# Last keys of a head pair in four 64x64 tiles with half of the queries each, sums side by side, three raw weights in the gates' buffers

## The chip, the cores and the metric

The kernel runs on one core of one Trainium2 chip. A core has TensorE (PE, matrix products; its weight loads are listed as PEld), VectorE (DVE), ScalarE (ACT), GpSimd (POOL) and SyncE (SP, which issues DMAs), all with their own instruction streams. The metric is the device time of one execution in microseconds (us); lower is better.

## The reference

All inputs and the output are float32 or float64 as given: B = 4 batches, H = 12 heads, S = 448 tokens, D = 64 per head; the three FFN weights arrive as 64-bit floats and the kernel converts them itself.

```python
scores = (1 / sqrt(D)) * q @ k.T                   # per batch and head
scores = cap * tanh(scores / cap)
attn = exp(scores - max); attn = attn / (sum(attn) + 1e-9)
x = (attn @ v) as [B * S, H * D]                   # 1792 x 768
out = ((x @ w_a) * (x @ w_b)) @ w_out              # 768 -> 1536 -> 768
```

## The kernel before

**Pairs.** Heads are done two at a time: a pair is head `hp` and head `hp + 6` of one batch, 24 pairs in all. The transposed keys and queries of one head of the pair lie on rows 0 to 63 (the 64 numbers of a head), those of the other on rows 64 to 127; `own` names these two row halves. The 448 keys of a head make three tiles of 128 (c = 0 to 2) and a rest of `R` = 64, the last keys (c = 3).

**A pair's steps.** `scores` (L258) puts keys against queries, so a score tile has keys on its rows and 448 queries along it: per full tile one 128-column matmul for each head (L266), for the last keys one 64x64 tile for each head, where the two heads share one 128-row result. `tanh` (L277) and `exp` (L285) run on ScalarE, one exp for tiles 0 and 1 (half 0) and one for tiles 2 and 3 (half 1). `attend` (L301) multiplies values by the exponentials: 64 columns of values for each head, over 128 keys; the last keys of both heads lie in one 128-row tile, and `vb` holds zeros where the other head's rows are. The softmax sums need a sum over keys: VectorE adds the tiles (`add_full`, L289), and `sums` (L320) lets TensorE add up the 128 rows with a matrix of ones, 64 queries at a time (`SC`), 14 small matmuls in four column groups of 32. For pairs 3 to 11 (`ON_PE`) the last keys' part of that is done by seven more such matmuls, `sums_last` (L310), right behind attend; for the other pairs VectorE does it (`add_last`, L296). `recip`, a round through DRAM (`store_rec`, `load_den`) and `scale` divide; `split_x` writes x as a high and a low part.

**Two phases.** Pairs 0 to 11 (phase one) are attention alone, in fp32. Pairs 12 to 23 (phase two) run between pieces of the FFN's first half (the tokens of batches 0 and 1); there keys and queries are split in a high and a low part (`turn_hi`, `turn_lo`), and each score tile is three products of the faster fp32r type (L271); the last keys are copied into two zero-padded 128x128 tiles `kz` by ScalarE (`last_keys`, L251) and take three products of 128x128 (L274). After pair 23 the second half of the FFN runs alone. A piece of FFN is `hidden` (L455, 18 matmuls: 6 row blocks by three products) or `project` (L486, 9 matmuls over three blocks of `w_out`); `gate` (L469) multiplies the two hidden results and splits the product into high and low, in buffers with the tags `gh` and `gl`, three of each. Two of those six are lent out until then as `den` buffers of pairs 10 and 11 (`LENT`).

**Weights.** Each block of 128 x 768 is loaded as 64-bit floats (`load64`, L385, two buffers tagged `w64`), converted in six steps (`conv`, L402: two on ScalarE L406 and L409, three on VectorE L411, L414, L417, one on GpSimd L420), then split into a high part (`split_hi`, L433, on ScalarE in the first half) and a low part (`split_lo`, L448, VectorE). The blocks go in the order a0, b0, a1, b1, a2, b2, o0, o1, o2, and so on; `t` counts them. The program's names are `wta` and `wtb` for the converted block, `wha`, `wla` for its parts.

**What sets the order.** TensorE's order is written out in `chain` (L637 to 703): per pair of phase one the scores of tiles 0 and 1, attend of the pair before, the scores of tiles 3 and 2, sums of the pair before that; in phase two attend, scores 0 and 1, sums, FFN work of half a `GAP` (20.4 us), scores 3 and 2, FFN work again. For the other engines a planner at the end places each step by a due time that it counts back from the chain (`due`), with planned costs in us that stand in each `job`. The lines touched by the change are in `load_v`, `last_keys`, `scores`, `tanh`, `add_last`, `attend`, `sums_last`, `sums`, `load_den`, `load64`, `split_hi`, `gate`, and in the code that makes the jobs.

Of the kernel before, what the change touches and what calls it, by code (L numbers as in the profile page):

```python
# [119 lines left out]
def kernel(  # L120
# [29 lines left out]
    SC = 64  # L150
# [5 lines left out]
    AHEAD = 4  # L156
    BLK = 32
# [12 lines left out]
    even.tile([P, 688], F32, tag="even", name="even")  # L170
# [22 lines left out]
    kz = [const.tile([P, P], F32R, tag=f"kz{x}", name=f"kz{x}") for x in "hl"]  # L193
    vb = [const.tile([P, 2 * NC3 + 2, D], F32, tag=f"vb{i}", name=f"vb{i}") for i in range(3)]

    own, krem = (slice(0, D), slice(D, P)), (S - R, 0)
# [25 lines left out]
    def load_v(pi, n):  # L222
        b, hp = divmod(pi, NP)
        t = vb[pi % 3]
        j = n % 2
        src = v[b, hp + j * NP]
        eng = nc.gpsimd if 3 <= pi < NPG else nc.sync
        if n < 2:
            rows = src[j * R : j * R + NC3 * P].rearrange("(c p) d -> p c d", p=P)
            eng.dma_start(t[:, j * (NC3 + 2) : j * (NC3 + 2) + NC3], rows)  # L230
        else:
            eng.dma_start(t[own[j], NC3 + j], src[krem[j] : krem[j] + R])
# [12 lines left out]
    def turn_lo(pi, nm):  # L245
# [3 lines left out]
        stk[nm, pi] = (hi, lo)  # L249

    def last_keys(pi):  # L251
        for z, x in zip(kz, stk["k", pi]):
            for j, o in enumerate(own):
                nc.scalar.copy(z[o, j * R : (j + 1) * R], x[o, krem[j] : krem[j] + R])
# [3 lines left out]
    def scores(pi, c):  # L258
        tk, tq = stk["k", pi], stk["q", pi]
        psc = ps_sc.tile([P, 2, 512], F32, tag="pssc", name=f"psc_{pi}_{c}")  # L260
        full = c < NC3
        if pi < NPG:
            for j, o in enumerate(own):
                at = j * R + c * P if full else krem[j]
                to = psc[:, j, :S] if full else psc[o, 0, :S]
                nc.tensor.matmul(to, tk[o, at : at + (P if full else R)], tq[o], start=True, stop=True)  # L266
        elif full:
            for x, y in products:
                for j, o in enumerate(own):
                    kk = tk[x][o, j * R + c * P : j * R + (c + 1) * P]  # L270
                    nc.tensor.matmul(psc[:, j, :S], kk, tq[y][o], start=(x + y == 0), stop=(x == 1))  # L271
        else:
            for x, y in products:
                nc.tensor.matmul(psc[:, 0, :S], kz[x], tq[y], start=(x + y == 0), stop=(x == 1))  # L274
        prob[pi, "s", c] = psc

    def tanh(pi, c):  # L277
# [18 lines left out]
    def add_last(pi):  # L296
        t, pf = psum[pi % 2], prob[pi, 1]
        for j, o in enumerate(own):
            nc.vector.scalar_tensor_tensor(t[o, j], pf[o, 2], capt[o, 2:3], t[o, j], op0=ALU.add, op1=ALU.add)

    def attend(pi, hf):  # L301
# [3 lines left out]
        for c in range(2 * hf, 2 * hf + 2):  # L305
            for j, o in enumerate(own):
                p = prob[pi, hf][:, 2 * (c % 2) + (j if c < NC3 else 0)]
                nc.tensor.matmul(t[o, :S], tv[:, j * (NC3 + 1) + (c if j == 0 else (c + 1) % (NC3 + 1))], p, start=(c == 0), stop=(c == NC3))  # L308

    def sums_last(pi):  # L310
        t, pf = pvs[pi], prob[pi, 1]
        for m in range(0, SUB, 2):
            for i in range(P // Q):
                c = 2 * i + m // 2
                if c < NSC:
                    to = t[i * Q : (i + 1) * Q, S : S + SC]
# [592 lines left out]
```

## Time and profile before

| | |
|---|---|
| three runs, us | median 720.1, from 717.47 to 720.37 |
| the profiled execution, us | 719.65 |
| its span in the trace, us | 717.5 |
| busy TensorE, us | 705.0 (98%) |
| busy VectorE / ScalarE / GpSimd, us | 427.7 / 347.3 / 112.4 |

Matmuls are pipelined and their ends are modelled, so TensorE's busy share overstates; the starts of instructions are to be used instead. An fp32 matmul has two records of TensorE in the trace for each matmul in the code (counts such as x8 for four). Names are those of the program with buffer numbers left out: `psc` is a score result, `pf` the exponentials, `pv` the result of attend (sums go into its last columns), `pha` and `phb` the two hidden results, `po` the projection's.

### The profile page before, as it was taken

What the parts mean: (1) busy time and instruction counts of PE and PEld (TensorE: products, weight loads), DVE (VectorE), ACT (ScalarE), POOL (GpSimd) and SP (SyncE); (2) the same over time, 40 slices, a digit from 0 to 9 for tenths busy, and PEclk for the clock granted to TensorE, in tenths of its full rate; (3) what the DMA queues carried; (4) which work ended last, traced back from release to release, by engine and by line L of the source; (5) the groups of instructions that cost most, each with busy time, mean ns of one, the idle gap of its engine ahead of it and who ended that gap; (6) DMA issues with size and microseconds to landing.
All of it is one profiled execution on the core that took longest, in us unless ns stands there. A gap on an engine that the chain in (4) does not pass through costs nothing.

```text
span 717.5 us, 11286 instructions
## 1 busy us (share of the span) xinstructions
PE 705.0 (98%) x4388; PEld 581.1 (81%) x4388; DVE 427.7 (60%) x651; ACT 347.3 (48%) x475; POOL 112.4 (16%) x104
## 2 busy tenths in 40 slices
PE   8999999999999999999999999999999999999996
PEld 4333367877877878878889779999999999999996
DVE  5777898867568689596795749342033434434232
ACT  6988987656866764686556530222321112202100
POOL 0445532222222222221231100000000000000000
PEclk9999999999999999999999999999999999999999
DMA  9997686775795678767654438331032003101012
GB/s 128 164 169 157 146 216 133 189 187 140 187 212 144 182 168 210 192 160 195 146 138 125 145 93 266 100 107 46 5 86 81 27 29 104 50 18 44 1 45 113
DMA packets 142597, 90.55 MB, mean 126 GB/s; under 512 B 107882, under 2 KB 128394, under 8 KB 142538
## 3 DMA queue, kind: packets, MB, share of 16 engines
q1 hardware_dynamic: 135786, 82.53, 46.3%
q0 software_dynamic: 3040, 6.79, 4.2%
q10 hardware_dynamic: 3712, 0.46, 0.5%
q8 instruction: 36, 0.59, 0.4%
q14 instruction: 23, 0.19, 0.1%
HBM read 67.24 MB, written 22.50 MB: 125 GB/s over the span
## 4 chain that ended last, share of the span: by engine, by line
PE 66%; DMA 13%; DVE 7%; ACT 7%; SPq 4%; issue 3%; POOL 1%; DVEq 0%; ACTq 0%; POOLq 0%
PE po L493 7%; PE po L495 7%; PE po L494 7%; PE pv L308 6%; PE pha L462 5%; PE pha L460 5%; PE pha L461 5%; PE phb L462 5%; PE phb L460 5%; PE phb L461 5%; PE psc L266 4%; DMA w64b<-in_moe_w_b_dram 3%; DMA w64o<-in_moe_w_out_dram 3%; DMA den<-rd 2%; ACT pf L283 2%
## 5 line engine op out<-in xcount | busy, mean ns | idle before, releaser
L493 PE MATMUL po<-who,gh 128*128 128x384 f32 x336 | 114.6, 341 | 2.6 <-ACT who L440 1.2
L494 PE MATMUL po<-wlo,gh 128*128 128x384 f32 x336 | 113.0, 336 | 0.6 <-DVE wlo L448 0.6
L495 PE MATMUL po<-who,gl 128*128 128x384 f32 x336 | 113.2, 337 | 0.1
L460 PE MATMUL pha<-xhi,wha 128*128 128x448 f32 x288 | 105.0, 365 | 0.0
L460 PE MATMUL phb<-xhi,whb 128*128 128x448 f32 x288 | 104.8, 364 | 0.0
L462 PE MATMUL pha<-xhi,wla 128*128 128x448 f32 x288 | 104.5, 363 | 0.0
L462 PE MATMUL phb<-xhi,wlb 128*128 128x448 f32 x288 | 104.5, 363 | 0.0
L461 PE MATMUL pha<-xlo,wha 128*128 128x448 f32 x288 | 104.3, 362 | 0.0
L461 PE MATMUL phb<-xlo,whb 128*128 128x448 f32 x288 | 104.2, 362 | 0.0
L283 ACT ACTIVATE pf<-psc,capt 128x896 f32<-128x896 f32 (+1 forms) x96 | 84.0, 909 | 17.4 <-PE psc L271 10.5
L308 PE MATMUL pv<-pf,vb 128*64 128x448 f32 x384 | 77.7, 546 | 0.8 <-ACT pf L287 0.8
L287 ACT ACTIVATE pf<-pf,capt 128x1792 f32<-128x1792 f32 (+1 forms) x48 | 77.2, 1608 | 0.8
L504 DVE TENSOR_TENSOR acc<-po,acc 128x384 f32<-128x384 f32 x84 | 46.2, 553 | 44.3 <-PE po L495 44.2
L493 PEld LDWEIGHTS po<-who,gh 128*128 128x128 f32 x336 | 63.6, 189 | 6.3 <-ACT who L440 1.5
L467 ACT COPY asb<-pha 128x448 f32<-128x448 f32 x48 | 25.5, 532 | 80.9 <-PE pha L462 80.9
L477 DVE TENSOR_TENSOR asb<-phb,asb 128x448 f32<-128x448 f32 x48 | 29.8, 621 | 58.5 <-PE phb L462 58.4
L494 PEld LDWEIGHTS po<-wlo,gh 128*128 128x128 f32 x336 | 63.7, 189 | 0.9 <-DVE wlo L448 0.8
L495 PEld LDWEIGHTS po<-who,gl 128*128 128x128 f32 x336 | 63.5, 189 | 0.4 <-DVE gl L482 0.4
L308 PEld LDWEIGHTS pv<-pf,vb 128*64 128x64 f32 x384 | 25.3, 136 | 45.3 <-issue 35.4
L479 ACT CAST gh<-asb 128x448 fp32r<-128x448 f32 x48 | 27.1, 564 | 69.1 <-DVE asb L477 68.7
L460 PEld LDWEIGHTS pha<-xhi,wha 128*128 128x128 f32 x288 | 53.9, 187 | 5.1 <-issue 0.6
L460 PEld LDWEIGHTS phb<-xhi,whb 128*128 128x128 f32 x288 | 53.9, 187 | 5.0 <-issue 1.2
(108 smaller groups left out, 1045.1 us busy)
## 6 DMA issues: line engine op xcount, KB each, us to landing
w64o<-in_moe_w_out_dram SPq DMA_DIRECT2D x24, 384.0 KB, 4.9
w64a<-in_moe_w_a_dram SPq DMA_DIRECT2D x18, 384.0 KB, 4.4
w64b<-in_moe_w_b_dram SPq DMA_DIRECT2D x18, 384.0 KB, 4.2
den<-rd SPq DMA_DIRECT2D x48, 112.0 KB, 3.9
out_dram<-acc SPq DMA_DIRECT2D x13, 384.0 KB, 3.8
wda<-wta SPq DMA_DIRECT2D x12, 384.0 KB, 6.3
wdb<-wtb SPq DMA_DIRECT2D x12, 384.0 KB, 5.5
wdo<-wto SPq DMA_DIRECT2D x12, 384.0 KB
```

The lines of the kernel that those rows point to most:

```text
L266: nc.tensor.matmul(to, tk[o, at : at + (P if full else R)], tq[o], start=True, stop=True)
L283: nc.scalar.activation(to, prob.pop((pi, "s", c))[:, :n, :S], AF.Tanh, scale=capt[:, 1:2])
L287: nc.scalar.activation(pf, pf, AF.Exp, scale=capt[:, 0:1])
L308: nc.tensor.matmul(t[o, :S], tv[:, j * (NC3 + 1) + (c if j == 0 else (c + 1) % (NC3 + 1))], p, start=(c == 0), stop=(c == NC3))
L460: nc.tensor.matmul(t[:, :S], wh[:, kk], xhi[:, kk, cs], start=(kk == 0), stop=False)
L461: nc.tensor.matmul(t[:, :S], wh[:, kk], xlo[:, kk, cs], start=False, stop=False)
L462: nc.tensor.matmul(t[:, :S], wl[:, kk], xhi[:, kk, cs], start=False, stop=(kk == NK - 1))
L477: nc.vector.tensor_mul(t, phs.pop(("b", h))[:, :S], t)
L493: nc.tensor.matmul(t[:, :HALF], gh[:, cs], wh, start=(f == fs[0]), stop=False)
L494: nc.tensor.matmul(t[:, :HALF], gh[:, cs], wl, start=False, stop=False)
L495: nc.tensor.matmul(t[:, :HALF], gl[:, cs], wh, start=False, stop=(f == fs[-1]))
L504: nc.vector.tensor_add(acc[:, ti, hs], t, acc[:, ti, hs])
```

## The change

- **Scores.** In phase one each full tile is now four 64x64 matmuls instead of two of 64x128 (row half by column half). The last keys are four 64x64 tiles too, in both phases: head j's 64 keys against the first 224 queries (`SH`) give rows 0 to 63 of the result's part j, and against the other 224 rows 64 to 127. In phase two these four are fp32 products from the unsplit keys and queries, which `stk` now keeps; `kz`, `last_keys` and its jobs are gone.
- **Attend, adds, tanh of the last keys** follow that layout: `vb` has two slots for each half of the queries, attend's last step is four matmuls of 224 columns instead of two of 448.
- **Sums.** `SC` is 56 instead of 64: `sums` has 16 matmuls, `sums_last` 8, and `sums_last` stands behind the scores of tile 2, next to `sums` of the pair before.
- **Weights.** `gh` and `gl` become one buffer of twice the length, tag `g`, three of them. Raw weights a0, b0 and a2 (t = 0, 1 and 4) are loaded into these before the gates need them, so the `w64` buffers have less to hold. The high parts of a0 and b0 are made on VectorE (`EARLY`). `LENT` is gone, so the `den` of pairs 10 and 11 wait for the two ordinary buffers.
- **Planner.** Planned costs and kinds follow (`sums_last` counts as `sums`). The turn of a phase-two pair waits for the scores of tile 3 of the pair before.

```diff
@@ constants @@
-    SC = 64
+    SH = S // 2
+    SC = 56
+    EARLY = 2
+    GRAW = (0, 1, 4)
...
@@ turn_lo, scores @@
-        stk[nm, pi] = (hi, lo)
+        stk[nm, pi] = (hi, lo, tt)
...
+        if c == NC3:
+            kk, qq = (t[-1] for t in (tk, tq)) if pi >= NPG else (tk, tq)
+            for i in range(2):
+                for j, o in enumerate(own):
+                    nc.tensor.matmul(psc[own[i], j, :SH], kk[o, S - R :], qq[o, i * SH : (i + 1) * SH], start=True, stop=True)
+        elif pi < NPG:
+            for i in range(2):
+                at = c * P + i * D
+                for j, o in enumerate(own):
+                    nc.tensor.matmul(psc[own[i], j, :S], tk[o, at : at + D], tq[o], start=True, stop=True)
...
@@ attend @@
+            for i in range(1 if c < NC3 else 2):
+                for j, o in enumerate(own):
+                    if c < NC3:
+                        nc.tensor.matmul(t[o, :S], tv[:, j * NC3 + c], prob[pi, hf][:, 2 * (c % 2) + j], start=(c == 0), stop=False)
+                    else:
+                        to = t[o, i * SH : (i + 1) * SH]
+                        nc.tensor.matmul(to, tv[:, 2 * (NC3 + i) + j], halves(prob[pi, 1][:, 2])[:, j], start=False, stop=(i == 1))
...
@@ load64, split_hi @@
+            if t in GRAW:
+                own_g = gp.tile([P, 2 * GT], F32R, tag="g", name=f"w64{nm}_{f}", bufs=GF)
+                wraw[t] = own_g[:, : 2 * DM].bitcast(I32).rearrange("p (n t) -> p n t", t=2)
...
-        if g and nm == "b":
+        if t < EARLY or g and nm == "b":
             nc.vector.tensor_copy(hi, wfull[t])
...
@@ turns, attend_of, the chain @@
+            free = [("scores", pi - 2, c) for c in range(SUB)] + [("lo", nm, pi - 1)] + [("scores", pi - 1, NC3)] * (pi > NPG)
...
-        if pi in ON_PE and 1 in halves:
-            on_pe(("sums_last", pi), 0.35, sums_last, (pi,))
...
+        if pi - 1 in ON_PE:
+            on_pe(("sums_last", pi - 1), 0.3, sums_last, (pi - 1,), [("exp", pi - 1, 1)])
         if pi > 1:
             sums_of(pi - 2)
```

The first place is TensorE in one pair of phase one (pair 5's scores). Before:

```order
L266 MATMUL psc_0_457<-tq_421,tk_413 128x448 x2
L266 MATMUL psc_1_467<-tq_421,tk_413 128x448 x2
L308 MATMUL pv_472<-pf_0_406,vb_175 64x448 x4
L308 MATMUL pv_472<-pf_1_436,vb_175 64x448 x4
L318 MATMUL pv_472<-pf_1_436,both 32x64 x7
L266 MATMUL psc_3_502<-tq_421,tk_413 64x448 x2
L266 MATMUL psc_2_509<-tq_421,tk_413 128x448 x2
L329 MATMUL pv_401<-psum_165,sel 32x64 x14
```

After:

```order
L267 MATMUL psc_0_578<-tq_499,tk_491 64x448 x4
L267 MATMUL psc_1_589<-tq_499,tk_491 64x448 x4
L309 MATMUL pv_596<-pf_0_518,vb_174 64x448 x4
L309 MATMUL pv_596<-pf_1_548,vb_174 64x448 x2
L312 MATMUL pv_596<-pf_1_548,vb_174 64x224 x4
L262 MATMUL psc_3_621<-tq_499,tk_491 64x224 x4
L267 MATMUL psc_2_630<-tq_499,tk_491 64x448 x4
L320 MATMUL pv_596<-pf_1_548,both 32x56 x8
L329 MATMUL pv_512<-psum_166,sel 32x56 x16
```

The small matmuls of `sums_last` moved from behind attend to directly ahead of `sums`, and all score tiles have 64 rows of result.

The second place is ScalarE, where the first steps of weight a0 (`w64a_0`, `wta_0`) stand between the tanh and exp steps. Before, in pair 7:

```order
L283 ACTIVATE pf_7_0_708<-psc_7_1_697,capt_132 128x896
L406 ACTIVATE w64a_0_419<-w64a_0_419 128x768
L287 ACTIVATE pf_7_0_708<-pf_7_0_708,capt_132 128x1792
L409 ACTIVATE wta_0_740<-w64a_0_419 128x768
L283 ACTIVATE pf_7_1_746<-psc_7_3_736,capt_132 128x448
```

After, in pair 9:

```order
L282 ACTIVATE pf_9_0_961<-psc_9_1_948,capt_132 128x896
L406 ACTIVATE w64a_0_450<-w64a_0_450 128x768
L286 ACTIVATE pf_9_0_961<-pf_9_0_961,capt_132 128x1792
L282 ACTIVATE pf_9_1_995<-psc_9_3_979,capt_132 128x448
L282 ACTIVATE pf_9_1_995<-psc_9_2_986,capt_132 128x896
L409 ACTIVATE wta_0_1035<-w64a_0_450 128x768
L286 ACTIVATE pf_9_1_995<-pf_9_1_995,capt_132 128x1344
```

The steps stand two pairs later. In the same way b0 moved from pair 8 to pair 10, a1 from pair 10 to pair 11.

The third place is VectorE at the end of phase one, up to the low part of b0 (`wlb_0_0`). Before, behind the second add of pair 10:

```order
L294 TENSOR_TENSOR psum0_165<-psum0_165,pf_10_1_991 128x896
L358 TENSOR_TENSOR den_7_984<-pv_7_783,den_7_984 128x448
L414 TENSOR_SCALAR wta_1_1021<-wta_1_1021 128x768
L374 CAST xhi_170<-den_7_984 128x448
L375 TENSOR_TENSOR xlo_171<-den_7_984,xhi_170 128x448
L448 TENSOR_TENSOR wlb_0_0_1080<-wtb_0_933,whb_0_0_1059 128x768
```

After, behind the first steps of pair 12 and the second add of pair 11:

```order
L250 TENSOR_TENSOR lq_12_1318<-tq_12_1226,hq_12_1289 128x448
L414 TENSOR_SCALAR wta_1_1277<-wta_1_1277 128x768
L293 TENSOR_TENSOR psum1_166<-psum1_166,pf_11_1_1244 128x896
L438 CAST whb_0_0_1342<-wtb_0_1142 128x768
L417 SCALAR_TENSOR_TENSOR wta_1_1277<-w64a_1_976,wta_1_1277 128x768
L448 TENSOR_TENSOR wlb_0_0_1373<-wtb_0_1142,whb_0_0_1342 128x768
```

The low part of b0 moved from pair 10's add to behind pair 11's, and its high part (`whb`) is now a step of VectorE.

## Rows read from the trace of the kernel before

**Rows 1.** The page: chain of work that ended last, share of the span by engine.

```profile
PE 66%; DMA 13%; DVE 7%; ACT 7%; SPq 4%; issue 3%; POOL 1%; DVEq 0%; ACTq 0%; POOLq 0%
```

**Rows 2.** Timeline, TensorE, one pair (start, duration, engine, line, operation, out<-in, shapes, count).

```profile
49.04 1.77 PE L266 MATMUL psc<-tq,tk 64*128 64x448 f32 x8
50.74 3.23 PE L308 MATMUL pv<-pf,vb 128*64 128x448 f32 x16
53.90 0.42 PE L318 MATMUL pv<-pf,both 128*32 128x64 f32 x14
54.26 1.92 PE L266 MATMUL psc<-tq,tk 64*64 64x448 f32 x8
56.11 0.65 PE L329 MATMUL pv<-psum,sel 128*32 128x64 f32 x28
56.68 0.65 PE L266 MATMUL psc<-tq,tk 64*128 64x448 f32 x2
```

**Rows 3.** Timeline, weight loads of that pair; brackets hold idle time and releaser.

```profile
51.17 0.14 PEld L308 LDWEIGHTS pv<-pf,vb 128*64 128x64 f32 x2 [0.23 <-issue]
51.55 0.14 PEld L308 LDWEIGHTS pv<-pf,vb 128*64 128x64 f32 x2 [0.23 <-issue]
...
55.15 0.30 PEld L266 LDWEIGHTS psc<-tq,tk 64*128 64x128 f32 x4 [0.70 <-ACT pf L287]
```

**Rows 4.** Timeline, ScalarE, at the start and in that pair.

```profile
8.10 1.91 ACT L283 ACTIVATE pf<-psc,capt 128x896 f32<-128x896 f32 x2 [1.75 <-PE psc L266]
...
21.22 1.89 ACT L283 ACTIVATE pf<-psc,capt 128x896 f32<-128x896 f32 x2
...
55.27 0.64 ACT L283 ACTIVATE pf<-psc,capt 128x448 f32<-128x448 f32 x1 [0.62 <-PE psc L266]
56.22 1.01 ACT L283 ACTIVATE pf<-psc,capt 128x896 f32<-128x896 f32 x1 [0.32 <-PE psc L266]
```

**Rows 5.** Timeline, ScalarE, first conversion step of weights a0 and b0.

```profile
60.37 0.92 ACT L406 ACTIVATE w64a<-w64a 128x768 int32<-128x768 uint32 x1
...
72.56 0.93 ACT L406 ACTIVATE w64b<-w64b 128x768 int32<-128x768 uint32 x1
```

**Rows 6.** Timeline, TensorE, two and one sums ahead of the first two FFN pieces.

```profile
94.72 1.09 PE L329 MATMUL pv<-psum,sel 128*32 128x64 f32 x56
95.74 0.48 PE L460 MATMUL pha<-xhi,wha 128*128 128x448 f32 x1
...
104.48 0.65 PE L329 MATMUL pv<-psum,sel 128*32 128x64 f32 x28
105.06 0.47 PE L460 MATMUL phb<-xhi,whb 128*128 128x448 f32 x1
```

**Rows 7.** Timeline, VectorE and ScalarE, steps at the end of phase one.

```profile
92.41 0.54 DVE L414 TENSOR_SCALAR wta<-wta 128x768 int32<-128x768 int32 x1
...
93.84 0.95 DVE L448 TENSOR_TENSOR wlb<-wtb,whb 128x768 fp32r<-128x768 f32 x1
...
97.73 0.59 ACT L242 CAST hq<-tq 128x448 fp32r<-128x448 f32 x1
...
99.61 0.61 DVE L248 TENSOR_TENSOR lq<-tq,hq 128x448 fp32r<-128x448 f32 x1
100.15 1.08 DVE L294 TENSOR_TENSOR psum<-psum,pf 128x896 f32<-128x896 f32 x1
```

**Rows 8.** Timeline, TensorE, last keys of a phase-two pair and what follows.

```profile
217.57 0.37 PE L274 MATMUL psc<-hq,kzh 128*128 128x448 f32 x1
...
218.27 0.47 PE L271 MATMUL psc<-hq,hk 64*128 64x448 f32 x2
```

**Rows 9.** TensorE in the first projection: timeline, then windows (busy, clock, DMA, GB/s).

```profile
162.75 0.44 PE L493 MATMUL po<-who,gh 128*128 128x384 f32 x1 [1.19 <-ACT who L440]
163.75 0.44 PE L494 MATMUL po<-wlo,gh 128*128 128x384 f32 x1 [0.55 <-DVE wlo L448]
...
160.00:168.00 8.00, 6.26 (x26) 5.44 (x23) 5.46 (x9) 6.62 (x10) 0.00 (x0) 0.79 0.65 182
```

More of the change, by code (lines that the diff above doesn't have):

```diff
@@ L192 @@
     acc = const.tile([P, NTI, DM], F32, tag="acc", name="acc")
-    kz = [const.tile([P, P], F32R, tag=f"kz{x}", name=f"kz{x}") for x in "hl"]
-    vb = [const.tile([P, 2 * NC3 + 2, D], F32, tag=f"vb{i}", name=f"vb{i}") for i in range(3)]
-    own, krem = (slice(0, D), slice(D, P)), (S - R, 0)
+    vb = [const.tile([P, 2 * NC3 + 4, D], F32, tag=f"vb{i}", name=f"vb{i}") for i in range(3)]
+    own = slice(0, D), slice(D, P)
     raw, stk, prob, pvs = {}, {}, {}, {}
@@ L260, in scores, with halves @@
         psc = ps_sc.tile([P, 2, 512], F32, tag="pssc", name=f"psc_{pi}_{c}")
[L261 to L267, printed above, removed]
+        if c == NC3:
[9 more added lines that the diff above has]
+        else:
             for x, y in products:
                 for j, o in enumerate(own):
[L270 to L274, printed above, removed]
+                    nc.tensor.matmul(psc[:, j, :S], tk[x][o, c * P : (c + 1) * P], tq[y][o], start=(x + y == 0), stop=(x == 1))
         prob[pi, "s", c] = psc
+    def halves(t):
+        return t.rearrange("p (j s) -> p j s", j=2)
     def tanh(pi, c):
@@ L297, in add_last @@
         t, pf = psum[pi % 2], prob[pi, 1]
-        for j, o in enumerate(own):
-            nc.vector.scalar_tensor_tensor(t[o, j], pf[o, 2], capt[o, 2:3], t[o, j], op0=ALU.add, op1=ALU.add)
+        for i, o in enumerate(own):
+            to = t[o, :, i * SH : (i + 1) * SH]
+            nc.vector.scalar_tensor_tensor(to, halves(pf[o, 2]), capt[o, 2:3], to, op0=ALU.add, op1=ALU.add)
     def attend(pi, hf):
@@ L353 @@
     xs, hold = {}, {}
-    LENT = {NPG - 2: "gh", NPG - 1: "gl"}
     def scale(pi):
@@ L558, in softmax @@
         job(("rd", pi), "SP", 0.7, store_rec, (pi,), [("recip", pi)], 3.0)
-        own_den = [p for p in range(pi) if p not in LENT]
-        free = [("x", own_den[-2])] if pi not in LENT and len(own_den) > 1 else []
+        free = [("x", pi - 2)] if pi > 1 else []
         for j in range(2):
@@ L692 @@
         attend_of(pi - 1)
+        if pi == NPG:
+            on_pe(("sums_last", pi - 1), 0.3, sums_last, (pi - 1,), [("exp", pi - 1, 1)])
         if pi < NPAIR:
@@ L794 @@
     for key in chain:
-        now = "ffn" if key[0] in ("hidden", "project") or (key[0] == "scores" and key[1:] >= (NPG, 3) and key[2] == 3) else key[0]
+        now = "ffn" if key[0] in ("hidden", "project") else "sums" if key[0] == "sums_last" else key[0]
         if now != kind:
```

86 lines of the change are left out of this document (34 added, 52 removed).

## The prediction

> **What bounds the kernel now.** I read the chain that ended last first: TensorE has 66% of it, the rest lies in pieces under 15% [rows 1]. So a gain has to come out of TensorE's own row, and I read that row by start times, since the ends of matmuls are modelled. The reader should take one pair of phase one from [rows 2]. From the start of its scores at 49.04 to that of the next pair at 56.68 it takes 7.64 us, in five groups without a wait: scores of tiles 0 and 1, 1.70; eight attend steps, 3.16; `sums_last`, 0.36; scores of tiles 3 and 2, 1.85; `sums`, 0.57. In that same pair ScalarE waits for scores twice, 0.62 and 0.32 us [rows 4]: TensorE is ahead of nothing there, it is the limit, and ScalarE has 0.94 us to spare. At the start it is the other way: ScalarE runs from 8.10 to 21.22 without a pause, two pairs in 13.12, so 6.56 a pair [rows 4]. That is the floor under any faster TensorE. In phase two TensorE waits for weights in a few places only; the worst is the first projection [rows 9].
>
> **What one group costs.** An fp32 matmul has two passes. In attend a pass starts every 0.38 us (51.17 to 51.55 [rows 3]); eight make 3.01 of the 3.16, so 0.15 us is lost where the tile shape changes. Scores with 128 columns on each 64-row half have four passes, 1.50, and take 1.70. The 64x64 scores of tile 3 take 0.89 for two passes, 0.14 over 0.75 (54.26 [rows 2] to 55.15 [rows 3]), like attend and not like the wide tiles. For sums, one alone takes 0.58 and two in a row take 1.02 (94.72 to 95.74, and 104.48 to 105.06 [rows 6]); so the second costs 0.44 for its eight steps of four tiles, 0.055 a step, and the change of shape 0.14.
>
> **The change, phase one.** Four tiles of 64x64 are not in the trace as a group. If all four run beside each other, as the two diagonal ones do, a pass of 448 columns stays at 0.38 and one of 224 costs 0.19 (on the line between 64 columns, 0.055, and 448, 0.376). If the two column halves of a row half take turns, each pass costs twice that. I take the first: two row halves beside each other (L266) and two column halves (L308) both show it, and nothing shows a limit on both at once.
> - Scores 0 and 1: four passes plus 0.16 for the change of shape and two more issues, 1.66 for 1.70: 0.04 less.
> - Scores 3 and 2: 2 x 0.19 + 2 x 0.376 + 0.16 = 1.29 for 1.85: 0.56 less; one change of shape falls away too, as tiles 3 and 2 now have the same.
> - `sums_last` beside `sums`: 24 matmuls for 21, but of 56 columns, in 12 steps at 0.049, plus 0.14: 0.73 for 0.93, so 0.20 less.
> - Attend: the last two passes become four of 0.19: nothing, at most 0.01 more.
> Together 0.80, so 6.84 us a pair, still over ScalarE's 6.56. In the slot of pair 3, where `sums_last` is not yet there, 7.29 (7.64 less 0.35) becomes 6.63.
>
> The start gains nothing, as ScalarE is the limit; it loses an estimated 0.3, half of a tanh of tile 3, since that of pair 0 now stands ahead of the exp that attend waits for. Tanh of pair 3 so starts at 21.22 + 6.56 + 0.3 = 28.1, that of pair 9 at 28.1 + 6.63 + 5 x 6.84 = 68.9. From there the conversions of weights stand in ScalarE's order, two instructions each (0.92 by the row, 0.8 each to the next start, so 1.6 [rows 5]): a0 in pair 9, b0 in pair 10, a1 in pair 11; before they stood two pairs earlier and used the 0.94 of spare time. Now ScalarE is the limit: exp of pair 10 ends at 68.9 + 2 x 6.56 + 2 x 1.6 = 85.2. Behind it TensorE has half an attend (1.58), scores 3 and 2 (1.29), and 20 steps of sums with a change of shape (1.12): the first FFN piece starts at 89.2. I take 89.5 for joints, against 95.74 [rows 6]: **6.2 us earlier**.
>
> **What is late next.** The second piece, phb, comes 9.3 us after the first [rows 6], at 98.8. Its weights must pass VectorE, whose order there has add and split steps of pairs 7 to 11 and now also the hi split of a0 and b0. Exp of pair 11 ends at 85.2 + 6.56 + 1.6 = 93.4; behind it ScalarE makes two hi parts of pair 12 (0.59 each by its row), so lq of pair 12 starts on VectorE at 94.6, and then come six steps up to wlb: lq 0.54 and add 1.00 (to the next start), a step of the shift's kind 0.54 and the hi split like it, L417 and L448 0.95 each [rows 7]. That is 4.52, so wlb is done at 99.1 with nothing lost at a handover. So phb waits 0.3 by the count; I take 0.9, since the pieces behind it have no slack either, and 5.3 us is left.
>
> **Phase two.** Tile 3 of scores was three 128x128 products, 0.70 us to the next group with its change of shape (217.57 to 218.27 [rows 8]), and had no change of shape ahead of it. Now there is one ahead (0.09) and four fp32 tiles of 224 columns: 0.09 + 2 x 0.19 + 0.14 = 0.61, 0.09 less. Sums of 8 steps at 0.049 instead of 0.055: 0.05 less. Twelve pairs: 1.6 us. The four copies of last keys a pair leave ScalarE; I count no gain for it, since TensorE's waits in the trace are for weights. The turn of the next pair now waits for the scores of tile 3 of the last one; half a `GAP` of FFN work (10.2 us as planned) and an attend lie between, and its chain is three steps of about 0.6 each.
>
> The first projection now stands idle 1.19 us for who and 0.55 for wlo, and the eight us around that have a granted clock of 0.79 of full speed on average, so the lower of its two levels (1.2 instead of 2.4 GHz) for part of them [rows 9]: 1.74 idle and 0.21 x 8 = 1.7 of clock, 3.4 us in all. Raw weights come earlier after the change (three more buffers), but demand comes 5 us earlier too, and the conversion of the second output weight stands later in ScalarE's order, behind exp of pair 14. Bounds: all 3.4 us gained, or as much lost again. I take 0.7 gained.
>
> **Sum.** The profiled execution took 719.65 with a span of 717.5, and the runs had a median of 720.1. 719.65 - 5.3 - 1.6 - 0.7 = **712.0 us**. The second half of the FFN is as it was.
>
> **A rule to weigh.** In attend the weight load of the next pass runs (0.14 us) while the current pass streams in the same 128 rows, and passes keep 0.38 apart [rows 3].
> The Trainium skill, TensorE: Matmul & The Clock Gate, Part 3 (The mechanism), says that a weight load overlaps running matmuls only when its row group differs. By that rule the column halves of one row half would each show their load. The trace disagrees for tiles of 128 rows; for four of 64x64 no run here shows it.
> If loads did show, eight passes a pair would each be 0.13 longer (a load of 64 columns on 64 rows lies near attend's 0.14), 12.8 us in twelve pairs: 724.8.
>
> **Rivals.**
> 1. *Conversions keep their length.* For: VectorE and ScalarE are full at the seam, and from its first ScalarE step [rows 5] to the end of its low part [rows 7] weight b0 took 22.2 us (72.56 to 94.79). With its start after the change at 79.0 (68.9 + 6.56 + 1.6 and two tanh, 1.9), b0 is done at 101.2, and phb waits 2.4 to 2.8, not 0.9; the backlog goes on to the first projection, which loses 3 more than now. That is 1.9 + 3.7 more than in the forecast: 717.6, within 0.5%. Against: much of those 22 us was lying idle for a due time.
> 2. *Column halves take turns* (ends slower). Place: the scores of phase one. Price: 0.75 for each of three tiles and 0.38 for the fourth, per pair 2.63, 31.6 in phase one and 4.5 in phase two, 748. It cancels the gain once a fifth of the passes are doubled. For: two streams of queries read the same 64 rows. Against: attend's two streams do so on 128 rows and hold 0.38.
> 3. *Loads show*, as above: 724.8.
> 4. *The change does not do what it says*, if four tiles or 56-column steps cost what the old ones did and only shape changes fall away (0.15 a pair in nine pairs, and nothing else): 718.
>
> **How the numbers follow.** Forecast 71%, rival 1 16%, rival 2 5%, rival 3 4%, rival 4 4%. About 0.5% (3.6 us) is what a measurement of this kernel can tell from no change, so faster means under 716.5. All but a little of the forecast is there: 0.70 faster; rivals 1 and 4 and that little make 0.20 within it; rivals 2 and 3, with some of a worse projection, 0.10 slower. The range reaches down to the forecast with the whole projection stall gone and the phb wait gone too, with joints 1 us better (712.0 - 2.7 - 0.9 - 1.0, about 707), and up past rivals 1 and 4 to 718.5.
>
> **What would show it.** Right: a pair of phase one in 6.8 to 6.9 us with scores 3 and 2 in 1.3; the first FFN piece at 89 to 90.5; the three old L274 products gone and about 0.6 in their place. Rival 2 shows as passes 0.75 apart, rival 3 as passes 0.5 apart, rival 1 as the same 6.8 a pair but phb waiting over 2 us for a DVE row and a longer gap at the first projection. I am wrong if ScalarE's waits of 0.62 and 0.32 are still there in pairs 4 to 8.

## The result, and the profile after

The changed kernel takes **707.66 us** (median of 4 runs, 705.91 to 709.79) against 719.88 beside it: a ratio of 0.9838, 95% interval 0.9803 to 0.9874, so 12 us less. The forecast was 712.0 with a range from 707.0 to 718.5. The profiled execution took 705.91 with a span of 704.1; it is the fastest of the four, and that matters below. Of all 15 executions of this program, 4 here and 11 beside the experiments, the middle one took 708.17.

First the chain that ended last, from the page of the changed kernel, to be held against [rows 1]:

```profile
PE 86%; issue 5%; POOL 3%; ACT 2%; DMA 2%; SPq 1%; ACTq 0%; DVE 0%; POOLq 0%
```

TensorE has gone from 66% to 86%, DMA from 13% to 2%. Most of the waits for data that stood in the chain are gone, which shorter matmul groups do not explain by themselves. A pair of phase one on TensorE, as in [rows 2] (start, duration, line, operation, shapes, count):

```profile
46.58 1.73 PE L267 MATMUL psc<-tq,tk 64*64 64x448 f32 x16
48.24 2.48 PE L309 MATMUL pv<-pf,vb 128*64 128x448 f32 x12
50.55 0.93 PE L312 MATMUL pv<-pf,vb 128*64 128x224 f32 x8
51.40 0.61 PE L262 MATMUL psc<-tq,tk 64*64 64x224 f32 x8
51.83 0.93 PE L267 MATMUL psc<-tq,tk 64*64 64x448 f32 x8
52.69 0.40 PE L320 MATMUL pv<-pf,both 128*32 128x56 f32 x16
52.91 0.58 PE L329 MATMUL pv<-psum,sel 128*32 128x56 f32 x32
53.42 0.61 PE L267 MATMUL psc<-tq,tk 64*64 64x448 f32 x4
```

By starts: 1.66 for tiles 0 and 1, 3.16 for attend, 1.29 for tiles 3 and 2, 0.73 for both kinds of sums, 6.84 in all, each to 0.01 as forecast. ScalarE's waits of 0.62 and 0.32 us in each pair [rows 4], whose return was the prediction's sign of being wrong, are gone: in pairs 4 to 8 it waits 0.12 at most. The end of phase one, first on TensorE, then on GpSimd and VectorE (the first FFN piece is `pha` at 89.03, against 95.74 in [rows 6]; `phb` follows), and last the reciprocal and the scale of pair 8 in the kernel before:

```profile
89.03 0.48 PE L460 MATMUL pha<-xhi,wha 128*128 128x448 f32 x1
...
94.01 2.48 PE L309 MATMUL pv<-pf,vb 128*64 128x448 f32 x12 [1.11 <-ACT asb L467]
...
99.46 0.48 PE L460 MATMUL phb<-xhi,whb 128*128 128x448 f32 x1
99.77 0.37 PE L461 MATMUL phb<-xlo,whb 128*128 128x448 f32 x1
100.14 0.47 PE L462 MATMUL phb<-xhi,wlb 128*128 128x448 f32 x1
```

```profile
80.54 1.85 POOL L420 TENSOR_TENSOR wta<-wta,w64a 128x768 int32<-128x768 int32 x1 [3.91 <-DVE wta L417]
...
80.73 2.16 DVE L371 TENSOR_TENSOR xlo<-den,xhi 128x448 fp32r<-128x448 f32 x1
...
83.11 0.50 DVE L337 RECIPROCAL rec<-rec 128x56 f32<-128x56 f32 x1
...
93.29 0.62 DVE L354 TENSOR_TENSOR den<-pv,den 128x448 f32<-128x448 f32 x1 [0.32 <-DMA den<-rd]
...
99.14 0.95 DVE L448 TENSOR_TENSOR wlb<-wtb,whb 128x768 fp32r<-128x768 f32 x1
```

```profile
87.85 0.55 DVE L337 RECIPROCAL rec<-rec 112x64 f32<-112x64 f32 x1
...
98.55 0.61 DVE L358 TENSOR_TENSOR den<-pv,den 128x448 f32<-128x448 f32 x1
```

Two things are to be seen. Attend of pair 11 waits 1.11 us. The row names ScalarE, but the exp of pair 11 had ended at 92.4; what ends at 93.91 is the scale of pair 8 (L354), which empties the buffer that attend writes into (in the code the results of pairs 8 and 11 share one), and attend starts 0.1 us later. That scale waits 0.32 us for its divisor, which goes from the reciprocal (done at 83.61) through DRAM and back; until then VectorE was busy with the 15 steps that stand between the two in its order. In the kernel before the scale was done at 99.16, 0.4 us ahead of attend at 99.55. And `phb` needs `wlb` for its third matmul: 0.37 instead of the usual 0.20 from 99.77 to 100.14.

The first projection runs through. Windows of it (busy per engine, clock, DMA share, GB/s), against the last row of [rows 9], and around it the load of weight a3 and the ScalarE rows, of the kernel before and then of the changed one:

```profile
154.50:162.50 8.00, 8.00 (x49) 7.82 (x46) 7.87 (x14) 7.07 (x12) 0.00 (x0) 1.00 0.96 216
```

```profile
153.06 1.34 SPq L397 DMA_DIRECT2D w64a<-in_moe_w_a_dram  x2
...
160.61 0.91 ACT L406 ACTIVATE w64a<-w64a 128x768 int32<-128x768 uint32 x1 [5.26 <-DMA w64a<-in_moe_w_a_dram]
...
161.88 0.83 ACT L440 CAST who<-wto 128x768 fp32r<-128x768 f32 x1
```

```profile
144.83 1.31 SPq L397 DMA_DIRECT2D w64a<-in_moe_w_a_dram  x2
...
151.14 0.91 ACT L406 ACTIVATE w64a<-w64a 128x768 int32<-128x768 uint32 x1
...
152.74 0.82 ACT L440 CAST who<-wto 128x768 fp32r<-128x768 f32 x1
```

Here the old stall begins. In the kernel before, ScalarE stood 5.26 us before the first step of weight a3, whose load had not landed, and the high part of the third output weight (`who`), which the projection waits for, was queued behind it. In the changed kernel the load of a3 is issued at 144.83 instead of 153.06, and ScalarE doesn't wait. The load needs the buffer of weight o1, free when GpSimd has converted that block: at 151.61 in the kernel before (two other transfers of SyncE still went ahead of the load), at 144.80 in the changed one.

**Where the 13.4 us between the two spans went**, by starts in both traces:

| place | before | after | gained up to here |
|---|---|---|---|
| first FFN piece | 95.74 | 89.03 | 6.7 |
| second piece, phb | 105.06 | 99.46 | 5.6 |
| third piece | 110.27 | 104.89 | 5.4 |
| first projection | 160.23 | 154.68 | 5.5 |
| end of that projection's first stretch | 173.67 | 164.26 | 9.4 |
| second half of the FFN | 429.31 | 415.80 | 13.5 |
| last matmul | 711.30 | 697.78 | 13.5 |

Of the 8.0 us behind the first projection's start, 3.9 are its own stretch, 2.7 are later stretches of projections, in which the kernel before has small stalls (0.4 to 0.7 us by starts, at 183, 186, 254, 270 and 340 us) and the changed kernel none, and the rest is attention in phase two.

### The profile page after: what moved, and what is told of

Its sections match the earlier page's. It is cut to its first block, busy times and chain, and to the rows that moved or that the text cites. A ratio compares the mean times of both kernels' runs of the same rounds, so it can differ in the third digit from the quotient of the medians.

```text
span 704.1 us, 12147 instructions
## 1 busy us (share of the span) xinstructions
PE 692.4 (98%) x4850; PEld 580.3 (82%) x4850; DVE 428.7 (61%) x651; ACT 336.1 (48%) x425; POOL 116.1 (16%) x108
## 4 chain that ended last, share of the span: by engine, by line
PE 86%; issue 5%; POOL 3%; ACT 2%; DMA 2%; SPq 1%; ACTq 0%; DVE 0%; POOLq 0%
PE po L492 9%; PE phb L460 8%; PE po L494 8%; PE po L493 8%; PE pha L460 8%; PE phb L462 8%; PE phb L461 8%; PE pha L461 8%; PE pha L462 8%; PE pv L309 4%; PE psc L271 4%; PE pv L312 1%; POOL vb L234 1%; PE pv L329 1%; ACT pf L282 1%
## 5 line engine op out<-in xcount | busy, mean ns | idle before, releaser
L492 PE MATMUL po<-who,g 128*128 128x384 f32 x336 | 113.3, 337 | 0.0
L494 PE MATMUL po<-who,g 128*128 128x384 f32 x336 | 112.4, 334 | 0.0
L493 PE MATMUL po<-wlo,g 128*128 128x384 f32 x336 | 112.2, 334 | 0.0
L492 PEld LDWEIGHTS po<-who,g 128*128 128x128 f32 x336 | 63.1, 188 | 1.8 <-DVE tk L239 0.6
L493 PEld LDWEIGHTS po<-wlo,g 128*128 128x128 f32 x336 | 63.1, 188 | 0.1
L494 PEld LDWEIGHTS po<-who,g 128*128 128x128 f32 x336 | 63.1, 188 | 0.0
L478 ACT CAST g<-asb 128x448 fp32r<-128x448 f32 x48 | 27.1, 565 | 73.4 <-DVE asb L476 73.1
L309 PE MATMUL pv<-pf,vb 128*64 128x448 f32 x288 | 59.6, 548 | 2.3 <-ACT pf L286 1.2
L462 PEld LDWEIGHTS phb<-xhi,wlb 128*128 128x128 f32 x288 | 54.0, 187 | 3.7 <-DVE wlb L448 0.4
```

The lines of the kernel that those rows point to most:

```text
L309: nc.tensor.matmul(t[o, :S], tv[:, j * NC3 + c], prob[pi, hf][:, 2 * (c % 2) + j], start=(c == 0), stop=False)
L462: nc.tensor.matmul(t[:, :S], wl[:, kk], xhi[:, kk, cs], start=False, stop=(kk == NK - 1))
L492: nc.tensor.matmul(t[:, :HALF], gh[:, cs], wh, start=(f == fs[0]), stop=False)
L493: nc.tensor.matmul(t[:, :HALF], gh[:, cs], wl, start=False, stop=False)
L494: nc.tensor.matmul(t[:, :HALF], gl[:, cs], wh, start=False, stop=(f == fs[-1]))
```

## The experiments

Each kernel was timed beside the kernel before on the same chip. The changed kernel itself ran twice more with them (0.9843 and 0.9834), so a ratio of about 0.984 is the standard; each ratio has an interval of some 0.002 to 0.004 to either side.

| kernel | median us | before | ratio, 95% interval |
|---|---|---|---|
| e1, no borrowed buffers | 713.67 | 718.01 | 0.9942, 0.9926 to 0.9958 |
| e2, high parts on ScalarE | 708.16 | 718.01 | 0.9852, 0.9827 to 0.9876 |
| e3, wide full tiles | 708.28 | 718.01 | 0.9857, 0.9840 to 0.9874 |
| e4, sums apart | 711.05 | 718.01 | 0.9895, 0.9877 to 0.9912 |
| e5, copies again | 707.36 | 719.62 | 0.9837, 0.9811 to 0.9862 |
| e6, changed kernel again | 708.53 | 719.62 | 0.9843, 0.9820 to 0.9867 |
| e7, one conversion step left out | 709.31 | 719.62 | 0.9867, 0.9843 to 0.9891 |
| e8, value loads by GpSimd | 707.15 | 719.62 | 0.9828, 0.9804 to 0.9851 |
| e9, two borrowed buffers | 714.19 | 719.41 | 0.9923, 0.9905 to 0.9941 |
| e10, reciprocal first | 709.91 | 719.41 | 0.9865, 0.9840 to 0.9891 |
| e11, reciprocal first, b0 on ScalarE | 710.74 | 719.41 | 0.9868, 0.9848 to 0.9888 |
| e12, changed kernel again | 708.27 | 719.41 | 0.9834, 0.9814 to 0.9855 |

### What took the projection's stall away: e1, e9 and e5

```diff
-    GRAW = (0, 1, 4)
+    GRAW = ()          # e1
...
+    GRAW = (0, 1)      # e9
```

> The changed kernel, with all raw weights in the two w64 buffers again. Theory 1 (the three borrowed buffers bring the raw loads forward, so that ScalarE no longer stands before the first step of a3 with the third output weight queued behind it): the load of a3 is issued over 3 us later than in the changed kernel's trace (144.8 us), ScalarE waits for it again, the first projection loses 2 to 4 us, and the time is 709.5 to 712. Theory 2 (the stall went because ScalarE has less to do, four copies of last keys a pair less): no stall comes back, 706 to 708.5.

> The changed kernel with two borrowed buffers (a0 and b0) instead of three. Theory 1 (each borrowed buffer brings the chain of raw loads forward by about one block, some 3 to 6 us): the load of a3 is issued between the 144.8 us of the changed kernel and the one of the kernel without borrowed buffers, and the first projection loses 0 to 4 us, 707.5 to 711. Theory 2 (two are enough, the third only moves work): no stall, 706.5 to 708.

e1 came out at 713.67, above the upper end that theory 1 gave, and the load of a3 is issued at 153.69 instead of 144.83. Its trace at the first projection, TensorE, the window around it, and the last conversion step and high part of the third output weight:

```profile
160.43 0.69 PE L492 MATMUL po<-who,g 128*128 128x384 f32 x1 [3.42 <-ACT who L440]
161.81 0.69 PE L493 MATMUL po<-wlo,g 128*128 128x384 f32 x1 [0.69 <-DVE wlo L448]
```

```profile
156.00:166.00 10.00, 5.89 (x21) 5.16 (x20) 9.77 (x15) 6.67 (x10) 1.84 (x1) 0.66 1.05 240
```

```profile
157.04 1.84 POOL L420 TENSOR_TENSOR wto<-wto,w64o 128x768 int32<-128x768 int32 x1 [3.38 <-ACT pf L282]
...
159.55 0.83 ACT L440 CAST who<-wto 128x768 fp32r<-128x768 f32 x1
```

The stall is back, and longer than it was: TensorE now arrives 4.5 us sooner than in the kernel before (155.69 to 160.23) at weights that come only 2.3 us sooner (`who` at 159.55 against 161.88). One half of theory 1 was not so: ScalarE does not wait for a3 here, `who` itself is late, because its last conversion step on GpSimd starts at 157.04, where the changed kernel has it at 150.32. Its raw load came late too: ScalarE waited 0.95 us for it at 151.03. So what the borrowed buffers bring forward is the whole chain of raw loads. The window has a granted clock of 0.66 on average, so for part of it the lower level (1.2 of 2.4 GHz), and the matmuls behind the wait start 0.32 apart instead of 0.17. By starts the projections of e1 lie 1.0 us behind the changed kernel's at the first matmul and 7.6 behind from the second projection on; nothing further is lost later.

e9 tells that two are not enough. With two, the time is that of e1 within the intervals, against theory 1, which had put it between, and theory 2, which saw no stall. The load of a2 (the third borrower) then waits for a buffer and is issued when GpSimd is through with its conversion:

```profile
102.97 1.27 POOL L397 DMA_DIRECT2D w64a<-in_moe_w_a_dram  x2 [0.30 <-POOL wta L420]
```

Its first projection, on TensorE (the wait for `wlo` that follows is 1.24):

```profile
160.19 0.44 PE L492 MATMUL po<-who,g 128*128 128x384 f32 x1 [2.34 <-ACT who L440]
```

Everything behind a2 in the two `w64` buffers shifts with it; its load of a3 is issued at 151.48. So buffers for a0 and b0 alone buy nothing here, and adding the one for a2 brings all of it; whether a2's alone would do was not run.

The five smaller stalls of the kernel before did not come back in e1. e5 asks whether the copies of last keys were their cause:

```diff
+        if pi >= NPG:
+            job(("z", pi), "ACT", 0.8, last_keys, (pi,), [("lo", "k", pi), ("scores", pi - 1, 3)])
...
+        ready = [...] + ([("z", pi)] if c == NC3 and pi >= NPG else [])
```

> The changed kernel, with the four copies of last keys a phase-two pair on ScalarE again, which nothing reads (the step is the one of the kernel before: four copies of 64x64, 0.24 us each, that the scores of tile 3 wait for). Theory 1 (the small stalls of the kernel before at 183, 186, 254, 270 and 340 us, 2.2 us in all, were collisions on ScalarE and VectorE that less work on ScalarE made rarer): stalls of 1 to 2.5 us in the projections come back, 707.5 to 709. Theory 2 (they hang on how the planner's order falls out, not on this load): none or others come, 706 to 707.

0.9837: no change, and no stall in any projection. Theory 2 stands as far as this goes: it is not these copies. Two of the five (183 and 186) lie behind another wait of 5.17 us of ScalarE for a raw weight in the kernel before; those at 254 and 270 stand behind VectorE steps; the one at 340 has no named wait. Since no single undone part brought them back, their cause is left open between the later raw loads and the planner's order.

### The matmul groups: e3 and e4

```diff
# e3: scores, full tiles of phase one
-            for i in range(2):
-                at = c * P + i * D
-                for j, o in enumerate(own):
-                    nc.tensor.matmul(psc[own[i], j, :S], tk[o, at : at + D], tq[o], start=True, stop=True)
+            for j, o in enumerate(own):
+                nc.tensor.matmul(psc[:, j, :S], tk[o, c * P : (c + 1) * P], tq[o], start=True, stop=True)
...
# e4: sums_last right behind attend
+        if pi in ON_PE and 1 in parts:
+            on_pe(("sums_last", pi), 0.3, sums_last, (pi,), [("exp", pi, 1)])
...
```

> The changed kernel, with the full key tiles of phase one as two matmuls of 64 rows by 128 columns again, the last keys left as four 64x64 tiles. By the trace of the changed kernel against the one before, tiles 0 and 1 cost 1.66 against 1.70, tile 2 alone 0.86 against 0.95, and one more change of shape comes between tiles 3 and 2 (0.09 to 0.14). Theory 1 (the gain of the scores is in the last keys, not in the full tiles): 0.2 to 0.3 us a pair in nine pairs, 2 to 2.5 us, 709.5 to 710. Theory 2 (ScalarE is so near that TensorE's time no longer shows): under 1 us, 707.5 to 708.5.

> The changed kernel, with the eight matmuls of sums_last right behind attend again. Two changes of shape more a pair, 0.09 to 0.14 in nine pairs: the pair takes 6.95 to 7.0 us instead of 6.84, 708.5 to 709. Rival: the wait for scores 3 and 2 is what ScalarE has left, nothing changes at the seam, 707.5 to 708.

In e3 the pair takes 7.09 instead of 6.84 (this trace, TensorE):

```profile
54.47 1.77 PE L265 MATMUL psc<-tq,tk 64*128 64x448 f32 x8
56.18 2.48 PE L307 MATMUL pv<-pf,vb 128*64 128x448 f32 x12
...
59.34 0.61 PE L262 MATMUL psc<-tq,tk 64*64 64x224 f32 x8
59.88 1.02 PE L265 MATMUL psc<-tq,tk 64*128 64x448 f32 x4
60.83 0.40 PE L318 MATMUL pv<-pf,both 128*32 128x56 f32 x16
...
61.56 0.65 PE L265 MATMUL psc<-tq,tk 64*128 64x448 f32 x2
```

That is 0.25 a pair, as theory 1 has it: 0.05 for tiles 0 and 1, 0.11 where tile 3 hands over to tile 2, 0.09 for tile 2. The first FFN piece comes 1.7 us later than in the changed kernel's profile. But the time is only 0.0014 to 0.0023 of the ratio higher, 1.0 to 1.7 us, with overlapping intervals, which leave room for theory 1's 2 to 2.5 as for theory 2's under 1; the pair's time is what is settled.

In e4 the pair takes 6.98, 0.14 more, as expected. Yet the time is 0.9895, some 4 us above the standard, against 1 to 1.3 expected. The first piece comes 3.5 us later than in the changed kernel's profile, 1.5 of that from a slower start (pair 3 begins at 27.77 instead of 26.24; in this execution the clock was at its lower level from 12.4 to 15.8 us), and 0.62 is a wait for the scale of pair 7, done at 92.42. Then attend of pair 11 waits 3.41 us, for the scale of pair 8 again:

```profile
99.05 0.62 DVE L354 TENSOR_TENSOR den<-pv,den 128x448 f32<-128x448 f32 x1
...
99.77 1.72 PE L309 MATMUL pv<-pf,vb 128*64 128x448 f32 x8 [3.41 <-issue]
```

So more of the loss lies in that wait than in the two changes of shape. VectorE is busy without a pause from 91.80 up to this scale, and among the steps ahead of it is `wlb`, done at 95.9 here and at 100.1, behind the scale, in the changed kernel. The planner has set another order, so e4's time is not the price of the changes of shape alone.

### The end of phase one: e2, e7, e8, e10, e11, and the changed kernel again

```diff
-    EARLY = 2
+    EARLY = 0          # e2; 1 in e11
...
# e7: conv
-        if step == 0:
+        if step == 0 and t < 2:
+            pass
+        elif step == 0:
...
# e8: load_v, and the engine of its jobs
-        eng = nc.gpsimd if 3 <= pi < NPG else nc.sync
+        eng = nc.gpsimd if 3 <= pi <= NPG else nc.sync
...
# e10 and e11: split_x of pair 6 behind the reciprocal of pair 8
-            job(("x", pi), "DVE", 0.9, split_x, (r,), [("scale", pi)])
+            job(("x", pi), "DVE", 0.9, split_x, (r,), [("scale", pi)] + [("recip", 8)] * (pi == 6))
```

> The changed kernel, with the high parts of a0 and b0 on ScalarE again (EARLY = 0). Theory 1 (ScalarE is the limit in pairs 9 to 11): each of the two steps puts 0.7 us on its row ahead of the end of exp of pair 11, the attend of pair 11 and what follows come 0.7 to 1.5 us later, 708.3 to 709.2. Theory 2 (VectorE's row is what the second piece waits for): the attend comes later, but wlb earlier, and it comes out even, 707 to 708.

e2 moved the wait. The first piece starts as early as in the changed kernel (89.25) but stands 1.55 us at its third matmul for `wla`, which VectorE's order has at 90.45 (ScalarE's high part was done at 86.89, and VectorE had no pause between), and its next nine matmuls start 0.37 apart, at the lower clock (0.50 from 91.5 to 94.9); phb comes 2.4 us later than in the changed kernel's profile. `wlb`, done at 100.6, is not earlier either, so neither theory had the place of the loss. The time, 0.9852, cannot be told from the standard.

> The changed kernel without the first conversion step of a0 and b0 on ScalarE (L406, 0.8 us each to the next start); the two weights come out as zero, which changes no duration. Theory 1 (ScalarE is the limit at the end of phase one, as the prediction has it, and the attend of pair 11 and phb follow from it): the first FFN piece comes 0.8 to 1.5 earlier, phb 0.8 to 1.5 earlier, 705 to 706. Theory 2 (the first piece follows ScalarE, but the attend of pair 11 waits for the scale of pair 8, whose divisor comes by way of DRAM, and phb for VectorE): the first piece comes earlier, the attend and phb do not, by more than 0.4, and the time stays within 0.5 of the changed kernel.

> The changed kernel as it is, as the standard for the runs beside it: 0.9838 of the kernel before, 706 to 707, with no stall of the first projection.

e7 takes 1.6 us from ScalarE (GpSimd's last step then subtracts the block from itself, and the planner counts 0.01 us for the step left out) and gains nothing (0.9867): against theory 1. Theory 2 is only partly borne out: the attend and `phb` are not earlier, but neither is the first piece, which comes at 89.24 against 89.03. TensorE waits 0.24 us for ScalarE ahead of pair 11's scores instead of 0.75, and then the first piece waits 0.74 for the scale of pair 7 on VectorE, which has no pause there. e7's attend of pair 11 waits too, and e6 and e12, the same program as the changed kernel, show that this wait is where executions differ. First piece and attend of pair 11 in e7 (TensorE; the scale of pair 8 ends there at 95.15), then attend and the scale ahead of it in e6 and e12 (VectorE and TensorE), and last the window around e12's attend:

```profile
89.24 0.47 PE L462 MATMUL pha<-xhi,wha 128*128 128x448 f32 x1 [0.74 <-DVE den L354]
...
95.25 4.08 PE L309 MATMUL pv<-pf,vb 128*64 128x448 f32 x12 [2.13 <-ACT wtb L411]
```

```profile
86.61 0.50 DVE L337 RECIPROCAL rec<-rec 128x56 f32<-128x56 f32 x1
...
96.50 0.62 DVE L354 TENSOR_TENSOR den<-pv,den 128x448 f32<-128x448 f32 x1
...
91.14 0.60 PE L329 MATMUL pv<-psum,sel 128*32 128x56 f32 x32 [1.44 <-DVE psum L293]
...
97.23 2.48 PE L309 MATMUL pv<-pf,vb 128*64 128x448 f32 x12 [1.67 <-ACT w64b L406]
```

```profile
83.84 0.50 DVE L337 RECIPROCAL rec<-rec 128x56 f32<-128x56 f32 x1
...
94.89 0.62 DVE L354 TENSOR_TENSOR den<-pv,den 128x448 f32<-128x448 f32 x1 [1.21 <-DMA den<-rd]
...
95.62 4.17 PE L309 MATMUL pv<-pf,vb 128*64 128x448 f32 x12 [2.67 <-ACT wtb L409]
```

```profile
95.60:99.80 4.20, 4.18 (x15) 1.82 (x17) 4.17 (x8) 0.00 (x0) 0.00 (x0) 0.59 0.81 184
```

From the end of the reciprocal to the start of that scale it takes 9.7 us in the changed kernel's profile, 9.4 in e6 and 10.6 in e12. Two things have to end there: the divisor's way through DRAM, and the 15 steps that VectorE has in between (16 in the kernel before). In these three the divisor comes last, but VectorE pauses for it only 0.32, 0.06 and 1.21 us; in e7, e8, e9 and the kernel before there is no pause, and the steps alone take 9.2 to 10.1. In e6 VectorE was late already (pair 11's scores come 1.0 us later than in the changed kernel's profile, the last sums of phase one wait 1.44 us for an add, and the first piece comes at 91.7). In e12 the wait is 2.67, and behind it the granted clock is 0.59 on average, so attend itself takes 4.9 us by starts instead of 3.2. The third piece comes at 108.1 in e6 and 107.9 in e12, 3 us later than in the changed kernel's profile; their spans are both 707.3 against 704.1, and from there on they run as it does, but for 0.3 us. So the gain at the end of phase one is 2.1 to 2.4 us in these two and 5.4 in that one. None of the three is the usual case: that profile is of the fastest of its four runs, those of e6 and e12 are of the slowest of theirs (709.11 and 709.08). If the times of the others differ at the same place, the middle execution (708.17, 2.3 above the fastest) gains some 3 us there; this is an estimate.

> The changed kernel with the value loads of pair 12 issued by GpSimd instead of SyncE, where they stand ahead of the store of pair 8's reciprocal (issued at 84.6, the reciprocal done at 83.6). Theory 1 (the attend of pair 11 waits for that way through DRAM): the scale of pair 8 and the attend of pair 11 come 0.5 to 1 us earlier than the 93.3 and 94.0 of the changed kernel; what phb gains of it is bounded by wlb, done at 100.1, so 0 to 0.4 us in all. Theory 2 (the wait is for exp of pair 11 on ScalarE, done at 92.4): the attend stays at 94.0, no change.

> The changed kernel, with the split of x of pair 6 (L370, L371, the second 2.16 us long there) behind the reciprocal of pair 8 in VectorE's order instead of ahead of it. Theory 1 (the attend of pair 11 waits for the scale of pair 8, and that for the reciprocal by way of DRAM): the scale of pair 8 comes 1 to 2 us earlier against the start of pair 11's scores (11.6 us behind it in the changed kernel's trace, 13.9 in its repetition), and so does the attend; phb is then held by wlb, so 0 to 1 us in all, 706.5 to 708. Theory 2 (VectorE's row is full, and the order within it is all the same): no change in the attend's distance, 707 to 708.5.

> As the kernel with the reciprocal of pair 8 ahead, and the high part of b0 on ScalarE again (EARLY = 1), where it stands behind the last exp of phase one. Theory 1 (at the seam VectorE is the limit): wlb comes 0.5 to 1 earlier, 706 to 707.5. Theory 2 (ScalarE is as full): no gain over the kernel beside it, within 0.7 us.

> The changed kernel as it is, a second time, as the standard for the runs beside it: 0.984 of the kernel before.

Both repetitions have the standard's ratio, e6 (708.53) with a median above the 706 to 707 expected. The three cures show no gain. In e8 the store goes out 0.02 us behind the reciprocal instead of 1.0, and yet the scale comes 9.2 us behind it, since VectorE's steps now set the length: it has no pause up to the scale. The scale comes at 95.7, 12.6 us behind the start of pair 11's scores (in that execution the reciprocal was done at 86.5, late on VectorE); the changed kernel's own profiles have 11.6, 13.9 and 13.2 (e6, e12), so this distance decides nothing. The time is the standard. In e10 the reciprocal of pair 8 is done 1.2 us earlier, at 82.4, but the split put behind it only moves VectorE's work to the stretch up to the scale, and the store stands in SyncE's queue behind three loads of values, up to 85.31:

```profile
82.75 1.71 SPq L231 DMA_DIRECT2D vb<-in_v_dram  x2
...
85.31 0.58 SPq L341 DMA_DIRECT2D rd<-rec  x1
...
89.69 0.47 SPq L348 DMA_DIRECT2D den<-rd  x1
...
94.61 0.62 DVE L354 TENSOR_TENSOR den<-pv,den 128x448 f32<-128x448 f32 x1 [0.16 <-DMA den<-rd]
```

The scale is 12.3 us behind pair 11's scores, within the changed kernel's own range, and the median, 709.91, lies above what either theory gave, with an interval that includes the standard. A kernel with less work on VectorE between reciprocal and scale, which is what these rows ask for, was not tried. e11 has wlb done at 101.6, not earlier, and a wait of 4.07 us by starts ahead of attend; theory 1 of it fell. No version beats the changed kernel beyond its interval.

## Why the prediction was right, and where it was not

- **A pair of phase one: right to 0.01 us**, group by group, for the reasons given: four 64x64 tiles run beside each other, and a pass of 448 columns keeps its 0.38 us. The sixteen records of L267 (four passes, with the change of shape) take 1.66 us, so passes are neither 0.75 nor 0.5 us apart, and rivals 2 and 3 fall; rival 4 falls with the groups' times. The rule of the Trainium skill (TensorE: Matmul & The Clock Gate, Part 3, The mechanism) is that a weight load overlaps running matmuls only when its row group differs. This trace disagrees for 64x64 tiles as well. (Rival 3's own numbers give 12.5 us, 8 x 0.13 x 12, and not 12.8; nothing hangs on it.)
- **The full tiles count more than I gave them.** I had 0.04 a pair for tiles 0 and 1 and named, without a size, the shape that tiles 3 and 2 now share; e3 puts 0.25 a pair on having the full tiles narrow: 0.05 for tiles 0 and 1, 0.11 for the shared shape, 0.09 for tile 2. The sum was right, since these were in its term for tiles 3 and 2.
- **First FFN piece: 89.5 forecast, 89.03 measured.** ScalarE's limit from pair 9 on shows as TensorE's wait for ScalarE ahead of pair 11's scores (0.75 us by its row). It is not the only limit there: with 1.6 us less on ScalarE (e7) the scale of pair 7 on VectorE holds the first piece to 89.24.
- **Second piece: the size fits one execution only, and the reason was not mine.** I took 0.9 us for wlb, and 5.3 left; the profile has 5.4. But the larger part of the loss is attend of pair 11 behind the scale of pair 8. I had moved TensorE's row forward by 6 us and left out that this scale moves less. The reciprocal starts 4.7 earlier than before (83.11 instead of 87.85), the scale 5.3 (93.29 instead of 98.55), the first piece 6.7; with the 0.4 us that attend had in hand, 1.0 is missing, and the row has a wait of 1.11. Between reciprocal and scale lie the divisor's way through DRAM and VectorE's 15 steps, some 10 us, and both have to end. Rival 1 had the full VectorE, but at `wlb`. In e6 and e12 this place and what goes with it (a late VectorE, a lower clock) cost some 3 us more. So this part of the forecast was too good by 3 us for those two, and by an estimated 2 for the middle execution; that it fits the profiled one is luck.
- **Rival 1's premise was right, its price was not.** b0 took 21.6 us from its first ScalarE step (78.47) to the end of wlb (100.09), nearly its 22.2. That phb waited only 0.17 for it is due to attend having waited 1.11 before; without that, phb would have stood some 1.3 us (an estimate, the two added). Its second half, 3 us more at the first projection, did not come: `who` was cast at 152.74, ahead of the projection at 154.68, and e1 and e9 show that without the three buffers it is late.
- **Phase two: 1.6 forecast, about 1.3 measured.** Tile 3 and what follows cost 0.54 instead of 0.70, sums 0.53 instead of 0.58, the added change of shape 0.09: 0.11 to 0.12 a pair.

```profile
103.26 0.36 PE L462 MATMUL phb<-xhi,wlb 128*128 128x448 f32 x1
103.55 0.61 PE L262 MATMUL psc<-tq,tk 64*64 64x224 f32 x8
104.09 0.47 PE L271 MATMUL psc<-hq,hk 64*128 64x448 f32 x2
```

- **First projection: the term that failed.** I took 0.7 gained, between bounds of 3.4 either way. It was 3.9, the whole stall and above the upper bound, and 2.7 more in stalls of later projections that my sum did not hold at all. I had read the stall in [rows 9] as a wait for `who` and `wlo` and stopped there. One step further back stands a load of a raw weight that had not landed, and behind that the two buffers. The diff gives the raw loads three more buffers, and e1 and e9 put 6 to 7.5 us on that. The kernel before with these buffers alone was not run, and what ended the 2.7 us of later stalls is not shown.

So the time came out at the range's lower end because two errors of opposite sign met: some 2 us too much at the end of phase one in the middle execution (3 in e6 and e12, none in the profiled one), and 5.9 too little at the projections (0.7 for 6.6). That the median lies inside the range is luck in this respect. The second error alone would have put the forecast's 712.0 at 706.1, below the range, and there the profiled execution is, with 705.91.

## What to carry to other kernels

Follow a stall back past the engine that it names, to the DMA and the buffer that the DMA waits for: what stands in an in-order queue behind a conversion waits for that conversion's load. A change that hands out buffers is to be priced at the stall that the late loads make, and it can act by a step: two buffers more gave nothing here, the third all of it. When one engine's row is moved forward, list the chains that don't move with it: a round trip through DRAM, and the order of a full engine. Curing one of two that end together (e8) gains nothing. And look at which of a kernel's executions a profile is of before its margins are called typical.

## What the runs showed of the hardware

- Four 64x64 fp32 tiles, two heads by two halves, run at once: 1.66 us for 16 records of 448 columns, four at a time at 0.38 and one change of shape, and 0.43 for 8 of 224 (51.40 to 51.83).
- A wait of 2.67 us on TensorE ahead of attend of pair 11 (e12) was followed by a granted clock of 0.59 on average over 4.2 us, and attend took 4.9 us for 3.2; after one of 1.11 us (the changed kernel) the clock stayed at 1.00. The length of the wait alone does not tell which comes: at the same place the clock fell to 0.50 for 3.4 us with 2.13 (e7) and 3.70 (e11), and stayed at 1.00 with 1.67 (e6), 1.79 (e10) and even 3.41 (e4), while in e2 it fell at a wait of 1.55 in the first piece. The cause is open.
- A VectorE subtraction of 128x448 took 2.16 us instead of the usual 0.62 while GpSimd's 128x768 add ran (80.54 to 82.39), and ended 0.5 us after it. The Trainium skill, SBUF — State Buffer, SBUF: two separate sides, has VectorE and GpSimd share a pair of ports that one instruction holds to its end; this trace agrees.
